# Retention attention and a gated convolution unit on one core: 64x64 inter-chunk products that open the output banks, joint chunk states, earlier weights and a new slot order

## The chip, the cores and the metric

The kernel runs on one core of a Trainium2 chip. The metric is the device time of one execution in microseconds (us), the median of several runs. The engines of the core are TensorE (PE in the profile, with its weight loads shown as PEld), VectorE (DVE), ScalarE (ACT), GpSimd (POOL) and SyncE (SP, which only issues transfers here).

## The reference

Inputs are q, k, v of shape (8 batches, 8 heads, 576 positions, 64), a value matrix and an output matrix of 512x512, and a causal convolution of five taps per channel. All are float32.

```python
scores = q @ k.T / sqrt(64)
Dmat   = where(i >= j, gamma[h] ** (i - j), 0)      # decay by distance, per head
attn   = (scores * Dmat) @ v                        # no softmax
x      = attn with the heads side by side           # (8, 576, 512)
gate   = sigmoid(sum over k of conv_w[k] * x shifted by k)
out    = (gate * (x @ w_val)) @ w_out
```

## The kernel before, in words

The decay is split into a factor on q and a factor on k by position, so the attention is linear attention with a causal mask. Each batch is cut into chunks of 128 positions. Within a chunk the kernel forms masked scores and multiplies them with v. Everything from earlier chunks is summed up in a running state, a 64x64 matrix per head (the sum of k-transposed times v), and reaches the chunk as one product of q with that state, the inter-chunk term.

The work is a list of 20 steps. Batches go in pairs, `u` from 0 to 3. Per pair there are five steps: two for the first batch and two for the second, each of 256 positions (two chunks, `x` = 0 and 1, with positions interleaved as `r` = 0 and 1), and one of 64 positions for both batches together, the remainder (`bb` is None). A step has these parts, each a function:

- `load` issues three transfers (k, q, v; 512 KB each) on SP's queue, four steps ahead. `cast` makes bfloat16 tiles `kb`, `qb`, `vb` with the decay factors multiplied in. It is called two steps ahead, and except at the start POOL does it (L199, L205).
- `transp` transposes kb and qb on PE (`tpk`, `tpq`, L218); ACT copies the first to `kt` (L224), DVE the second to `qt` (L222).
- `scores` (L242) are 64x64 products into PSUM tiles `sc`; DVE multiplies by the mask into `am` (L249). It is called for two groups of head pairs.
- `values` (L303) multiplies am with vb into two output banks `o`, one per chunk.
- `state` (L266) forms `ds`, the step's addition to the state, one call per chunk. `state_sum` adds it to the running sum `sn` on DVE (L281, L283), and ACT casts it to `wst` (L286). wst holds a head pair as a 128x128 block with zeros off the diagonal, so each of ACT's casts fills one half of the partitions and there are two per chunk.
- `inter` (L317) is the inter-chunk term: 128x128 products of wst with qt, added to the o banks after values has opened them.
- `evac` copies o to the layout `xt` (or `xr` for remainders) on ACT (L342, L335).

When a batch's 512 positions are done, they form a block for the second half: `conv` (L375, 160 products of 32x32 tiles with the diagonals `diag` in four PSUM tiles, then four sigmoids `gt` on ACT, L382), four pieces `val` (L390, `vps`, and DVE's product `zt`, L392) and four pieces `outp` (L397, `ops`, ACT's copy `ob`, L400, and a store on SP's queue). The remainders of two pairs make one block of 256. The last batch is given as two blocks of 256.

The order on each engine is the order of the program text; nothing is reordered later. The pieces of blocks wait in the list `work`. Between the parts of a step the program calls `fill(us)`, which adds to a credit and then takes pieces while the credit is at least half of the next piece's cost; the credit is capped at 4.0. A convolution is taken only where `fill` allows it. Transposes, states, convolutions, projections and outputs share one PSUM pool of four banks, `glp` with the tag "gps"; scores have two banks (`scp`) and the outputs o two (`opp`).

The full step of before, in program order:

```python
scores(s, ga); fill(0.9); transp(s + 1); scores(s, gb)
values(s, ga); inter(s, ga); fill(2.2, True)
state(s + 1, 0); values(s, gb); state(s + 1, 1); inter(s, gb)
evac(s); state_sum(s + 1, 0); state_sum(s + 1, 1); fill(1.8)
```

The start issues step 0's loads, makes constants, issues three more steps' loads, casts step 0, then calls `load_weights` (the convolution's taps `cw` as five transfers on ACT's queue, the two matrices on POOL's queue, converted to bfloat16 in the transfer) and casts step 1. `prep_weights`, called in step 1, builds the diagonals on DVE and rearranges the value matrix on ACT.

Of the kernel before, what the change touches and what calls it, by code (L numbers as in the profile page):

```python
# [31 lines left out]
def kernel(  # L32
# [14 lines left out]
    P = 128  # L47
# [14 lines left out]

    cst = ctx.enter_context(tc.tile_pool(name="cst", bufs=1))
# [82 lines left out]
    wtmp = cst.tile([P, DT, DM], BF16)  # L146
    wval = cst.tile([P, DT, NQ, P], BF16)
    wout = cst.tile([P, NQ, DM], BF16)

    def load_weights():  # L150
        with nc.allow_non_contiguous_dma(reason="conv"):
            for kk in range(KC):
                nc.scalar.dma_start(out=cw[:, kk, :],
                                    in_=moe_conv_w[kk].rearrange("(do di) -> di do", di=P))
        nc.gpsimd.dma_start(out=wtmp, in_=moe_w_val.rearrange("(do di) dp -> di do dp", di=P))
        for c in range(DT):
            nc.gpsimd.dma_start(
                out=wout[c * Q:(c + 1) * Q],
                in_=moe_w_out[c * P:(c + 1) * P, :].rearrange("(r x) n -> x r n", x=Q))

    def prep_weights():

        nc.vector.tensor_tensor(idr, ident[:, 0:Q], ident[:, Q:2 * Q], op=ALU.add)
        for i in range(2, NQ):
            nc.vector.tensor_tensor(idr, idr, ident[:, i * Q:(i + 1) * Q], op=ALU.add)
        nc.vector.tensor_copy(cwh, cw)
        nc.vector.tensor_tensor(cwl, cw, cwh, op=ALU.subtract)
        shp = [P, KC * DT, Q]
        for p2, w in ((0, cwh), (1, cwl)):
            nc.vector.tensor_tensor(  # L170
                diag[:, p2].rearrange("p k c x -> p (k c) x"),
                idr.unsqueeze(1).to_broadcast(shp),
                w.rearrange("p k c -> p (k c)").unsqueeze(2).to_broadcast(shp), op=ALU.mult)
        for do in range(DT):
            nc.scalar.copy(wval[:, do].rearrange("p r (c x) -> p r c x", x=Q),
                           wtmp[:, do].rearrange("p (c r x) -> p r c x", r=NQ, x=Q))


    wst = []
    for i in range(8):  # L180
        w = cst.tile([P, HP, 2, D], BF16, tag=f"wst{i}", name="wst")
        nc.vector.memset(w, 0.0)
        wst.append(w)


    def cast(s):
        u, bb, n = steps[s]
        r = st[s]
        R = 1 if bb is None else 2
        shp = [P, R, H, D]  # L190
        f0 = n * 2
        nb = 2 if bb is None else 4
        kb = cs.tile(shp, BF16, tag=f"kb{R}", name="kb", bufs=nb)
        qb = cs.tile(shp, BF16, tag=f"qb{R}", name="qb", bufs=nb)
        vb = cs.tile(shp, BF16, tag=f"vb{R}", name="vb", bufs=nb)

        for dst, src, f, eng in ((kb, r["kf"], fk, nc.gpsimd),
                                 (qb, r["qf"], fq, nc.vector if s == 0 else nc.gpsimd)):
            eng.tensor_tensor(dst, src.rearrange("p h r d -> p r h d"),  # L199
                              f[:, f0:f0 + R, :].unsqueeze(3).to_broadcast(shp), op=ALU.mult)  # L200
        vsrc = r["vf"].rearrange("p h r d -> p r h d")
        if s < 2:
            nc.scalar.copy(vb, vsrc)
        else:
            nc.gpsimd.tensor_copy(vb, vsrc)  # L205
        r.update(qb=qb, kb=kb, vb=vb)

    def transp(s):
        if s >= NS:
            return  # L210
        r = st[s]
        R = 1 if steps[s][1] is None else 2
        for nm in ("k", "q"):
            src = r[nm + "b"]
            tp = glp.tile([P, HP, R, P], BF16, tag="gps", name="tp" + nm)
            for hp in range(HP):
                for rr in range(R):
                    nc.tensor.transpose(tp[:, hp, rr, :],  # L218
                                        src[:, rr, 2 * hp:2 * hp + 2, :].rearrange("p a d -> p (a d)"), ident)
            t = at.tile([P, HP, R, P], BF16, tag=f"{nm}t{R}", name=nm + "t")  # L220
            if nm == "q":
                nc.vector.tensor_copy(t, tp)  # L222
            else:
                nc.scalar.copy(t, tp)  # L224
            r[nm + "t"] = t
# [30 lines left out]
    def state(s, x):  # L256
        if s >= NS or steps[s][1] is None:
            return
        u, bb, n = steps[s]
        r = st[s]  # L260
        ds = glp.tile([P, HP, D], F32, tag="gps", name="ds")
        for hp in range(HP):
            for rr in range(2):
                for hh in range(2):
                    h = 2 * hp + hh
                    nc.tensor.matmul(ds[HS[hh], hp, :], lhsT=r["kb"][HS[x], rr, h, :],  # L266
                                     rhs=r["vb"][HS[x], rr, h, :],
                                     start=(hp == 0 and rr == 0), stop=True, skip_group_check=True)
        r[("ds", x)] = ds

    def state_sum(s, x):
# [3 lines left out]
        ds = st[s][("ds", x)]  # L275
        m = 2 * n + x

        w = wst[6 + bb] if m == 2 * NSC - 1 else wst[m + 3 * bb]
# [6 lines left out]
        for hh in range(2):  # L285
            nc.scalar.copy(w[HS[hh], :, hh, :], sn[HS[hh]])  # L286
        wcur[(u, bb, m + 1)] = w

    xts = {}
    xrs = {}  # L290

    def values(s, hps):
# [3 lines left out]
        if "o" not in r:  # L296
            r["o"] = [opp.tile([P, HP, R * HF], F32, tag="o", name="o") for _ in range(2)]
        o = r["o"]
        for a, hp in enumerate(hps):
            for rj in range(R):  # L300
                for hh in range(2):
                    for x in range(2):
                        nc.tensor.matmul(o[x][HS[hh], hp, :], lhsT=r["vb"][HS[x], rj, 2 * hp + hh, :],  # L303
                                         rhs=r[("am", hps[0], hh)][HS[x], a, rj, :],
                                         start=(hp == 0 and rj == 0), stop=True, skip_group_check=True)

    def inter(s, hps):
        u, bb, n = steps[s]
        r = st[s]
        R = 1 if bb is None else 2  # L310
        o = r["o"]
        for x in range(2):
            key = (u, x, 2 * NSC) if bb is None else (u, bb, 2 * n + x)
            if key not in wcur:
                continue
            for hp in hps:
                nc.tensor.matmul(o[x][:, hp, :].rearrange("p (r i) -> p r i", r=R),  # L317
                                 lhsT=wcur[key][:, hp].rearrange("p a d -> p (a d)"),
                                 rhs=r["qt"][:, hp, :, HS[x]],
                                 start=False, stop=True, skip_group_check=True)  # L320

    def evac(s):
# [13 lines left out]
        else:  # L336
            if u not in xts:
                xts[u] = xp.tile([P, DT, 2, PAD + NSC * SC], BF16, name="xt")
                nc.gpsimd.memset(xts[u][:, :, :, 0:PAD], 0.0)
# [7 lines left out]
    work = []  # L347

    def push_block(xt, bi, t0, segs):
# [35 lines left out]
        def val(d):  # L385
            if d == 0:
                z[0] = zp.tile([P, DT, N], BF16, tag=f"z{N}", name="zt")
            vp = glp.tile(shape, F32, tag="gps", name="vps")
# [5 lines left out]
        def outp(m):  # L394
            op = glp.tile([P, DM], F32, tag="gps", name="ops")
# [22 lines left out]
    def fill(us, conv_ok=False):  # L418

        credit[0] = min(credit[0] + us, 4.0)  # L420
# [6 lines left out]

    for s in range(1, LOOK):
        load(s)
    cast(0)  # L430
    load_weights()
    cast(1)
    transp(0)
    for x in range(2):
        state(0, x)
        state_sum(0, x)
    for s in range(NS):
        u, bb, n = steps[s]
        last = u == B // 2 - 1
        if s == 1:  # L440
            prep_weights()
# [4 lines left out]
        if bb is None:  # L446
            hps = list(range(HP))
            scores(s, hps)
            fill(0.9)
            transp(s + 1)  # L450
            values(s, hps)
            state(s + 1, 0)
            state(s + 1, 1)
            inter(s, hps)
            evac(s)
            state_sum(s + 1, 0)
            state_sum(s + 1, 1)
            fill(4.0, True)
        else:
            ga, gb = list(range(HP // 2)), list(range(HP // 2, HP))  # L460
            scores(s, ga)
            fill(0.9)
            transp(s + 1)
            scores(s, gb)
            values(s, ga)
            inter(s, ga)
            fill(2.2, True)
            state(s + 1, 0)
            values(s, gb)
            state(s + 1, 1)  # L470
            inter(s, gb)
            evac(s)
            state_sum(s + 1, 0)
            state_sum(s + 1, 1)
            fill(1.8)
        b = 2 * u + (bb or 0)
        if bb is None:
            if u % 2 == 1:
                push_block(xrs[u // 2], None, 0, [(b - 2 + j, NSC * SC, REM) for j in range(4)])
        elif last and bb == 1:  # L480
            push_block(xts[u], bb, n * SC, [(b, n * SC, SC)])
        elif n == NSC - 1:
            push_block(xts[u], bb, 0, [(b, 0, NSC * SC)])
# [32 lines left out]
```

## Time and profile before

| | |
|---|---|
| time, median of three runs | 229.23 us (227.87 to 231.61) |
| span of the profiled execution | 228.7 us |
| instructions | 9242 |
| read from and written to device memory | 30.42 MB and 9.44 MB |
| share of 16 transfer engines, loads and stores | 62.4% |
| tap transfer (cw), packets | 2640 for 0.01 MB |
| convolution products (L375) | 1760 with their weight loads |
| inter products (L317) | 128 |

A line of a timeline gives the start, the time from first start to last end, the engine, the source line, the operation and its tiles, the count, and in square brackets the idle time before it and what ended it. A line of waits gives the engine and line that waited, what released it, and then the total, the number of times and the longest. PEld and PE overlap.

### The profile page before, as it was taken

Reading aid. Unit: us, or ns where it says so; the run is one execution under the profiler, and the core shown is the slowest. Engines: PE = TensorE matmul, PEld = TensorE weight load, DVE = VectorE, ACT = ScalarE, POOL = GpSimd, SP = SyncE. Lnnn points to the kernel's source line nnn. Section 1 sums busy time; section 2 is a strip of 40 time slices with the busy share of each in tenths; the row PEclk is TensorE's granted clock in tenths of the full one; section 3 lists DMA queues with packets and bytes.
Section 4 is the critical chain, followed back from the end, with each engine's and each line's share of the span. In section 5 each row is a group of like instructions: output and inputs, shape, how many; then the busy total and the mean of one; then the engine's idle time right before and its main releaser. Section 6 shows DMA issues by size and latency. Waiting matters only on the chain.

```text
span 228.7 us, 9242 instructions
## 1 busy us (share of the span) xinstructions
PE 170.9 (75%) x4160; PEld 108.0 (47%) x4160; DVE 101.0 (44%) x189; ACT 115.1 (50%) x228; POOL 89.4 (39%) x84
## 2 busy tenths in 40 slices
PE   0505769589799867997997958993899788894981
PEld 0404558145554743563565543553456554462560
DVE  3602885164275723733853605530476617320220
ACT  5107648366646737493484645283247736541331
POOL 3951676681783087067602750087500000000000
PEclk9999956999999999999999995899799979999798
DMA  6999999996991899669449995069404000312024
GB/s 168 290 220 229 278 202 242 286 264 224 257 202 56 242 311 285 184 209 269 81 140 268 307 259 141 0 212 304 92 20 167 3 6 0 143 47 95 3 95 92
DMA packets 71622, 39.39 MB, mean 172 GB/s; under 512 B 16800, under 2 KB 66976, under 8 KB 71584
## 3 DMA queue, kind: packets, MB, share of 16 engines
q1 hardware_dynamic: 67840, 37.76, 62.4%
q0 software_dynamic: 1104, 1.05, 2.7%
q8 instruction: 32, 0.52, 1.0%
q10 hardware_dynamic: 2640, 0.01, 0.7%
q14 instruction: 6, 0.05, 0.1%
HBM read 30.42 MB, written 9.44 MB: 174 GB/s over the span
## 4 chain that ended last, share of the span: by engine, by line
PE 58%; DVE 13%; ACT 10%; issue 9%; DMA 5%; SPq 3%; ACTq 0%; DVEq 0%
PE vps L390 14%; PE cps L375 13%; PE ops L397 12%; DMA vf<-in_v_dram 5%; DVE am L249 4%; PE sc L242 4%; PE o L303 4%; DVE zt L392 3%; PE o L317 3%; PE tpk L218 3%; PE tpq L218 3%; PE ds L266 3%; SPq L97 3%; ACT xt L342 2%; ACT gt L382 2%
## 5 line engine op out<-in xcount | busy, mean ns | idle before, releaser
L392 DVE TENSOR_TENSOR zt<-gt,vps 128x512 bf16<-128x512 f32 (+1 forms) x44 | 25.9, 590 | 69.8 <-PE vps L390 69.5
L199 POOL TENSOR_TENSOR kb<-kf,fk 128x1024 bf16<-128x1024 f32 (+1 forms) x20 | 34.6, 1730 | 40.4 <-DMA kf<-in_k_dram 27.6
L249 DVE TENSOR_TENSOR am<-sc,mask_c 128x512 bf16<-128x512 f32 x64 | 41.1, 684 | 16.5 <-PE sc L242 16.4
L390 PE MATMUL vps<-xt,wval 128*128 128x512 bf16 (+1 forms) x144 | 35.1, 383 | 7.4 <-ACT gt L382 4.3
L375 PE MATMUL cps<-xt,diag 32*32 32x512 bf16 (+1 forms) x1440 | 27.9, 380 | 16.0 <-issue 11.9
L397 PE MATMUL ops<-wout,zt 128*128 128x512 bf16 x144 | 37.5, 389 | 1.5 <-DVE zt L392 1.5
L400 ACT COPY ob<-ops 128x512 f32<-128x512 f32 x36 | 20.6, 590 | 33.4 <-PE ops L397 24.2
L382 ACT ACTIVATE gt<-cps 128x512 f32<-128x512 f32 (+1 forms) x44 | 19.4, 524 | 34.7 <-PE cps L375 34.7
L375 PEld LDWEIGHTS <-diag 32*32 32x32 bf16 x1760 | 21.7, 89 | 27.0 <-issue 23.8
L199 POOL TENSOR_TENSOR qb<-qf,fq 128x1024 bf16<-128x1024 f32 (+1 forms) x19 | 32.7, 1721 | 2.7 <-DMA qf<-in_q_dram 2.3
L342 ACT CAST xt<-o 128x512 bf16<-128x512 f32 x32 | 21.7, 751 | 13.7 <-PE o L317 7.1
L242 PE MATMUL sc<-qt,kt 64*64 64x128 bf16 (+1 forms) x576 | 18.1, 239 | 13.6 <-ACT kt L224 9.1
L390 PEld LDWEIGHTS <-wval 128*128 128x128 bf16 x176 | 17.0, 101 | 22.3 <-issue 12.9
L286 ACT CAST wst<-sn 64x256 bf16<-64x256 f32 x64 | 25.8, 403 | 1.0
L333 POOL COPY xr<-xt 128x32 bf16<-128x32 bf16 x4 | 0.8, 210 | 59.9 <-ACT xt L342 59.9
L224 ACT COPY kt<-tpk 128x1024 bf16<-128x1024 bf16 (+1 forms) x20 | 18.6, 932 | 10.7 <-PE tpk L218 10.4
L242 PEld LDWEIGHTS <-kt 64*64 64x64 bf16 x576 | 11.0, 117 | 24.1 <-issue 11.9
L397 PEld LDWEIGHTS <-zt 128*128 128x128 bf16 x144 | 13.2, 100 | 17.3 <-DVE zt L392 5.7
L303 PE MATMUL o<-am,vb 64*64 64x128 bf16 (+1 forms) x576 | 17.9, 231 | 2.9 <-issue 1.3
L218 PE MATMUL tpk<-ident,kb 128*128 128x128 bf16 x144 | 13.0, 239 | 7.9 <-POOL kb L199 7.9
L205 POOL CAST vb<-vf 128x1024 bf16<-128x1024 f32 (+1 forms) x18 | 16.9, 941 | 3.1 <-DMA vf<-in_v_dram 1.9
L218 PEld LDWEIGHTS <-kb 128*128 128x128 bf16 x144 | 10.4, 108 | 11.7 <-POOL kb L199 7.9
(46 smaller groups left out, 144.9 us busy)
## 6 DMA issues: line engine op xcount, KB each, us to landing
kf<-in_k_dram SPq DMA_DIRECT2D x16, 512.0 KB, 5.9
qf<-in_q_dram SPq DMA_DIRECT2D x16, 512.0 KB, 6.8
vf<-in_v_dram SPq DMA_DIRECT2D x16, 512.0 KB, 7.6
out_dram<-ob SPq DMA_DIRECT2D x32, 256.0 KB, 2.4
kf<-in_k_dram SPq DMA_DIRECT2D x8, 128.0 KB, 6.0
qf<-in_q_dram SPq DMA_DIRECT2D x8, 128.0 KB, 5.3
vf<-in_v_dram SPq DMA_DIRECT2D x8, 128.0 KB, 3.8
out_dram<-ob SPq DMA_DIRECT2D x8, 128.0 KB, 3.2
```

Source lines behind the costliest of these rows:

```text
L199: eng.tensor_tensor(dst, src.rearrange("p h r d -> p r h d"), f[:, f0:f0 + R, :].unsqueeze(3).to_broadcast(shp), op=ALU.mult)
L218: nc.tensor.transpose(tp[:, hp, rr, :], src[:, rr, 2 * hp:2 * hp + 2, :].rearrange("p a d -> p (a d)"), ident)
L242: nc.tensor.matmul(sc[hh][HS[x], a, rj, :].rearrange("p (r i) -> p r i", r=R), lhsT=r["kt"][HS[hh], hp, rj, HS[x]], rhs=r["qt"][HS[hh], hp ...
L249: nc.vector.tensor_tensor(am, sc[hh], mk.rearrange("p j i x -> p j (i x)").unsqueeze(1).to_broadcast(shp), op=ALU.mult)
L286: nc.scalar.copy(w[HS[hh], :, hh, :], sn[HS[hh]])
L303: nc.tensor.matmul(o[x][HS[hh], hp, :], lhsT=r["vb"][HS[x], rj, 2 * hp + hh, :], rhs=r[("am", hps[0], hh)][HS[x], a, rj, :], start=(hp == ...
L342: nc.scalar.copy(xts[u][:, :, bb, t0:t0 + P].rearrange("p a (i r) -> p a r i", r=R), o[x].rearrange("p a (r i) -> p a r i", r=R))
L375: nc.tensor.matmul(fold(cps[r][c * Q:(c + 1) * Q]), lhsT=diag[rs, p2, kk, c, :], rhs=win(c, kk)[rs], start=(kk == 0 and p2 == 0), stop=(kk ...
L382: nc.scalar.activation(gt, cps[r], AF.Sigmoid)
L390: nc.tensor.matmul(fold(vp), lhsT=wval[:, do, d, :], rhs=win(do, PAD), start=(do == 0), stop=(do == DT - 1))
L392: nc.vector.tensor_tensor(z[0][:, d, :], g[d], vp, op=ALU.mult)
L397: nc.tensor.matmul(op, lhsT=z[0][:, d, m * P:(m + 1) * P], rhs=wout[:, d, :], start=(d == 0), stop=(d == DT - 1))
```

## The change

Six things change together.

1. The state goes to bfloat16 as it is, without zero blocks: one cast of 128 partitions per chunk into a tile `w`. The inter-chunk term becomes 64x64 products, two per head pair and chunk, and it comes before `values`, so that it opens the output banks where a state exists.
2. `state` forms both chunks' additions in one call, with the products of both chunks alternating.
3. The taps come in one transfer on POOL's queue, and the diagonals are built on POOL, both ahead of the first cast. The two matrices come as float32 on SP's queue right behind step 0's loads, into tiles of the load pool, and are converted by ACT (`wval`) and POOL (`wout`).
4. Step 0 casts k on DVE, and step 1 casts v on POOL.
5. The parts of a step follow lists of slots. A letter is a part, a number is a `fill`, and "C" takes a convolution if one is next. The first batch is given as two blocks of 256.
6. The credit is capped at 2.0. After the last step, projections and outputs use the PSUM banks of scores and of o.

```diff
+    TPS, DSS, CAP = False, False, 2.0
...
-    wtmp = cst.tile([P, DT, DM], BF16)
...
+    with nc.allow_non_contiguous_dma(reason="conv"):
+        nc.gpsimd.dma_start(out=cw.rearrange("p k c -> p (k c)"),
+                            in_=moe_conv_w.rearrange("k (do di) -> di (k do)", di=P))
+
+    nc.gpsimd.tensor_tensor(idr, ident[:, 0:Q], ident[:, Q:2 * Q], op=ALU.add)
...
+    nc.gpsimd.tensor_copy(cwh, cw)
+    nc.gpsimd.tensor_tensor(cwl, cw, cwh, op=ALU.subtract)
...
     def load_weights():
-        with nc.allow_non_contiguous_dma(reason="conv"):
-            for kk in range(KC):
-                nc.scalar.dma_start(out=cw[:, kk, :],
-                                    in_=moe_conv_w[kk].rearrange("(do di) -> di do", di=P))
-        nc.gpsimd.dma_start(out=wtmp, in_=moe_w_val.rearrange("(do di) dp -> di do dp", di=P))
...
+        for half in range(2):
+            t = ld.tile([P, 2, DM], F32, tag="qf2" if half else "kf2", name="wvf", bufs=4)
+            nc.sync.dma_start(out=t, in_=moe_w_val[half * 2 * P:(half + 1) * 2 * P, :]
+                              .rearrange("(do di) dp -> di do dp", di=P))
+            wf[half] = t
...
     def prep_weights():
...
         for do in range(DT):
             nc.scalar.copy(wval[:, do].rearrange("p r (c x) -> p r c x", x=Q),
-                           wtmp[:, do].rearrange("p (c r x) -> p r c x", r=NQ, x=Q))
...
+                           wf[do // 2][:, do % 2].rearrange("p (c r x) -> p r c x", r=NQ, x=Q))
+        for half in range(2):
+            nc.gpsimd.tensor_copy(wout[:, 2 * half:2 * half + 2], wf[2 + half])
...
-        for dst, src, f, eng in ((kb, r["kf"], fk, nc.gpsimd),
+        for dst, src, f, eng in ((kb, r["kf"], fk, nc.vector if s == 0 else nc.gpsimd),
...
-        if s < 2:
+        if s == 0:
             nc.scalar.copy(vb, vsrc)
...
-    def state(s, x):
+    def state(s):
...
+                for x in range(2):
+                    for hh in range(2):
+                        h = 2 * hp + hh
+                        nc.tensor.matmul(ds[x][HS[hh], hp, :], lhsT=r["kb"][HS[x], rr, h, :],
+                                         rhs=r["vb"][HS[x], rr, h, :],
+                                         start=(hp == 0 and rr == 0), stop=True, skip_group_check=True)
...
-        for hh in range(2):
-            nc.scalar.copy(w[HS[hh], :, hh, :], sn[HS[hh]])
+        nc.scalar.copy(w, sn)
...
+    def inter(s):
...
+        for hp in range(HP):
+            for x in range(2):
+                for hh in range(2):
+                    if keys[x] in wcur:
+                        nc.tensor.matmul(r["o"][x][HS[hh], hp, :].rearrange("p (r i) -> p r i", r=R),
+                                         lhsT=wcur[keys[x]][HS[hh], hp, :], rhs=r["qt"][HS[hh], hp, :, HS[x]],
+                                         start=(hp == 0), stop=True, skip_group_check=True)
...
+    def gps(shape, name):
+
+        pools = [(glp, "gps")] if tail[0] is None else [(scp, "sc"), (opp, "o")]
...
-        credit[0] = min(credit[0] + us, 4.0)
+        credit[0] = min(credit[0] + us, CAP)
...
+    load_weights()
     for s in range(1, LOOK):
         load(s)
     cast(0)
-    load_weights()
+    transp(0)
+    state(0)
+    for x in range(2):
+        state_sum(0, x)
+    prep_weights()
     cast(1)
...
+    FIRST = ["I", "Sa", "Sb", "0.0", "Vb", "Va", "E", "B", "C", "X", "XS", "5.85", "T"]
+    FULL = [["I", "0.0", "Sa", "C", "T", "Va", "Sb", "5.4", "Vb", "X", "E", "B", "XS", "7.2"],
+            ["C", "I", "Sa", "X", "4.95", "XS", "Sb", "0.45", "T", "Va", "Vb", "E", "1.35", "B"]]
+    PART = ["X", "I", "Sr", "4.95", "T", "3.05", "Vr", "XS", "E", "B", "C"]
```

In the lists I is `inter`, Sa, Sb and Sr are `scores` for the first two head pairs, the last two and all four, Va, Vb and Vr are `values` in the same way, T is `transp` of the next step, X and XS are `state` and `state_sum` of the next step, E is `evac`, and B puts a finished block in the list. FULL[0] and FULL[1] are for a batch's first and second step, PART for remainders and FIRST for step 0.

## The prediction

> **What bounds the kernel now.** I read the page's busy shares first, then the table of windows, then the waits of PE, then the timeline of the start.
>
> ```profile
> PE 170.9 (75%) x4160; PEld 108.0 (47%) x4160; DVE 101.0 (44%) x189; ACT 115.1 (50%) x228; POOL 89.4 (39%) x84
> ...
> PE 58%; DVE 13%; ACT 10%; issue 9%; DMA 5%; SPq 3%; ACTq 0%; DVEq 0%
> ```
>
> PE leads, and the chain that ended last runs through it for 58% of the span. The rest of the chain is hand-overs to DVE and ACT, and 9% "issue". The windows (columns: length; busy time of PE, PEld, DVE, ACT, POOL; granted clock; DMA share; GB/s) split the span at landmarks: first scores, first 512-wide convolution (38.0), second one (58.0), fourth, sixth, tail.
>
> ```profile
> 0.00:19.95 19.95, 2.89 (x48) 2.30 (x49) 6.26 (x17) 6.00 (x21) 11.03 (x22) 1.00 1.03 224
> 19.95:38.00 18.05, 14.58 (x305) 11.84 (x306) 14.02 (x26) 12.38 (x23) 12.32 (x10) 0.74 1.06 234
> 38.00:58.03 20.03, 16.23 (x410) 9.68 (x410) 8.48 (x17) 11.34 (x21) 11.26 (x8) 0.98 0.94 260
> 58.03:101.40 43.37, 36.70 (x910) 22.54 (x908) 22.52 (x41) 26.05 (x50) 22.62 (x19) 1.00 0.83 218
> 101.40:154.10 52.70, 44.44 (x1088) 27.17 (x1088) 23.93 (x43) 28.17 (x55) 24.06 (x19) 0.94 0.70 187
> 154.10:200.10 46.00, 37.36 (x859) 22.48 (x858) 20.69 (x36) 23.44 (x44) 8.14 (x9) 0.93 0.33 93
> 200.10:228.70 28.60, 18.65 (x554) 11.95 (x552) 5.06 (x12) 7.77 (x20) 0.00 (x0) 0.90 0.22 66
> ```
>
> Three regimes. Up to 38 us the transfers are full (share 1.03, 1.06) and PE starves. From 58 to 200 PE is about 84% busy and no other engine is near it. In the tail everything is one chain. The timeline of the start shows why PE starves:
>
> ```profile
> 8.85 9.05 ACTq L153 DMA_DIRECT2D cw<-in_moe_conv_w_dram  x5
> ...
> 17.94 1.04 ACT L203 CAST vb<-vf 128x1024 bf16<-128x1024 f32 x1 [8.05 <-DMA cw<-in_moe_conv_w_dram]
> 18.89 1.01 ACT L224 COPY kt<-tpk 128x1024 bf16<-128x1024 bf16 x1
> 19.80 1.66 ACT L286 CAST wst<-sn 64x256 bf16<-64x256 f32 x4
> 19.95 0.40 PEld L242 LDWEIGHTS <-kt 64*64 64x64 bf16 x16 [9.27 <-ACT kt L224]
> ```
>
> ACT spends 9 us issuing five transfers of 4-byte elements and then casts step 1's values, so step 0's kt copy, ready since 8.9, waits. Then the diagonals (L163 to L170) sit on DVE from 25.72 to 29.4, ahead of the masking that PE needs (PE gap of 3.13 us). For 58 to 200 the waits of PE (total, times, longest) are:
>
> ```profile
> PE cps L375 <- issue: 8.5, 6, 4.3
> PE vps L390 <- ACT gt L382: 3.1, 5, 0.7
> PE cps L375 <- ACT kt L224: 2.5, 3, 1.2
> PE vps L390 <- ACT xt L342: 2.3, 3, 0.8
> PE ops L397 <- DVE zt L392: 1.5, 4, 0.5
> ```
>
> [...]
>
> **The change, part by part.**
>
> *Start.* Step 0's three loads land at 5.2, 7.0 and 8.8 us (issue plus landing), one per 1.8 us. The weights now follow as 2 MB of float32 on the same queue, four times a 512 KB load: to 16.0. Step 1's loads land at 17.8, 19.6 and 21.3 (before: 10.7, 12.4, 17.5). Step 0 no longer waits for ACT: kb and qb both on DVE (2 x 1.79) end at 9.5, transposes at about 10.6, and its scores and values finish near 17, not 25. But the state of step 1 (X) stands ahead of the first block's projection in PE's order, so PE is then gated by POOL, which serves in order: cw, diagonals, two wout copies, then kb, qb, vb of step 1. cw is the unknown: 2560 elements of 4 bytes, now one transfer issued by POOL at 5.8. Before, they took from 8.85 to 24.7 (17.5 + 7.2), 15.9 us; that is the upper bound (lands 21.7). Below, POOL's issue time by the wtmp and wout rows (0.94 us for 512 rows, 0.54 for 128, so some 3.1 for 2560) plus their own packet time (0.7% of the span, 1.6 us) and about as much latency: 11. I take 17, since the queue beside it is full. The diagonals on POOL cost 2 x 1.2 (1.90 us x 640/1024) plus 0.4: ready at 14, 19.8 or 24.5. wout copies 2 x 0.94, not before 16.0: done at 17.9, 21.7, 26.4. kb, qb, vb are 1.9 + 1.9 + 1.04: X at 22.8, 26.5, 31.3. From X to the first 512-wide convolution I add: projection 2 x 1.9, output 2 x 1.8, one 256-wide convolution 2.4, transposes 4.5, scores 2.9, values 2.9, states 4 x 0.58, inter 1.5, together 23.9, plus 3 for the cold clock and 2 of waits: 29. It starts at 51.7, 55.4 or 60.2, against 58.0. Taken: **2.6 saved** (6.3 to -2.2).
>
> *States at once.* Two calls of 16 cost 0.33 + 0.40 us of weight loads, one call of 32 costs 0.49 (99.87): 0.25 x 4 steps = 1.0 us per batch pair. *Inter as 64x64.* Sixteen weight loads take 0.26 us, the eight 128-wide ones 2 x 0.23: little by itself[...]. Over three pairs from 58 to 200: **4 saved**.
>
> *w without zero halves.* 64 casts of 0.403 us on ACT become 32 of about 0.4: 13 us of ACT. ACT is 50% busy, so this is worth only what stood behind it: kt, which the convolution waited for (2.5).
>
> *Slot order.* Between scores and the values that need them stand now a transpose, a projection or an output. Waits other than "issue" and gt sum to 9.9 (2.5 + 2.3 + 1.5 and nine rows under 0.8); I take 8 as gone. The gt wait (3.1) stays: where T follows C, the transposes need the PSUM buffers that gt frees. Against it: 1.5 for such buffer waits in new places. The clock of 0.94 and 0.93 lost 0.06 x 52.7 + 0.07 x 46 = 6.4[...]. PE's rows grow from 8322 to 8930 (256 for inter, 352 for the first block cut in two), 7% more to fetch: 0.8. **8 - 1.5 + 3 - 0.8 = 8.7 saved.** CAP 2.0 lets a fill place two or three pieces, yet PE's printed order still leaves three 256-wide blocks for the tail, as before.
>
> *Tail.* Projections and outputs use other PSUM pools, so the next convolution doesn't wait for ob: 0.50 + 0.46 in the timeline. **0.9 saved.** The memset of xt moving to the start, and DVE's eight wst memsets (2.19 us, before its data lands) cost nothing: DVE waits for the loads there.
>
> Sum 2.6 + 4 + 8.7 + 0.9 = 16.2; 229.2 - 16.2 = **213**.
>
> **Rivals.** *Late cw*: the upper bound holds, 4.8 us worse: 218. For it: the old transfers ran 16 us beside the same queue. Against: one transfer, started earlier. *All waits go*: early cw (6.3), work 4, all 9.9, all 6.4 of clock, tail 1.5: 201. For it: no engine but PE is over 61% busy in 58 to 101. Against: the transfers would need about 9.4 MB per 38 us, 248 GB/s, close to what the start reaches. *No change*: late cw (-2.2), work 4 and tail 0.9 saved, 2.3 of new costs and no wait gone: 229. *Slower*: the same, but C followed by T costs a microsecond at each of nine convolutions in place of 1.5 in all: 229.2 + 2.2 - 4 - 0.9 + 9 + 0.8 = 236. For it: one gps pool of four serves transposes, states, projections and convolutions.
>
> **How the numbers follow.** Forecast 0.47, late cw 0.18, all waits 0.20, no change 0.07, slower 0.08. The range 201 to 225 leaves out the last two and the far side of the third. Faster by over 2% (below 224.6) is the first three: 0.85; within 2% 0.07; slower 0.08.
>
> **What would show it.** Right: first scores by 14 us, the cast of step 1 on POOL starting between 18 and 26, the first 512-wide convolution near 55, about 40 us per batch pair, no wait of cps on kt, clock above 0.95. Wrong: POOL idle on cw beyond 24 us, transposes waiting for gt by over a microsecond per block, or "issue" gaps well above the 8.5 us of before.

## The result and the profile after

The changed kernel takes 217.05 us, the median of four runs (215.82 to 222.73), against 228.56 for the kernel before on the same chip: a ratio of 0.949, 95% interval 0.939 to 0.959. In a later set of runs it was 0.952 (0.945 to 0.960). The forecast was 213 us, range 201 to 225. Medians and ranges are over all runs of a kernel; a ratio and its interval leave out runs more than 1.5% above its fastest, and none is given where only one run is left. The profiled execution spans 214.0 us (before: 228.7). The two spans differ by 14.7 us and the medians by 11.5, because the profiled run of before was slower than its median and this one faster.

The first line below is from the page's busy times, the others from the table of windows (columns as before), cut at the same landmarks: three pieces of the start, up to the second batch's 512-wide convolution at 59.4, then the steps pair by pair, then the tail.

```profile
PE 165.8 (77%) x4464; PEld 107.6 (50%) x4464; DVE 97.7 (46%) x181; ACT 97.7 (46%) x199; POOL 93.1 (43%) x85
```

```profile
0.00:26.00 26.00, 9.19 (x289) 6.87 (x293) 7.60 (x16) 11.66 (x32) 14.96 (x27) 1.00 1.04 243
26.00:38.70 12.70, 11.10 (x224) 8.30 (x224) 7.16 (x14) 5.91 (x10) 10.82 (x8) 1.00 1.04 239
38.70:59.40 20.70, 14.75 (x467) 11.21 (x466) 9.30 (x19) 7.90 (x15) 13.85 (x11) 0.89 1.05 282
59.38:101.40 42.02, 37.34 (x942) 22.76 (x938) 22.90 (x41) 21.12 (x39) 21.32 (x17) 0.93 0.81 220
101.38:143.00 41.62, 35.65 (x1005) 23.04 (x1005) 21.85 (x40) 20.18 (x40) 19.71 (x14) 0.96 0.82 208
143.00:187.35 44.35, 39.74 (x1019) 23.99 (x1024) 23.87 (x42) 23.13 (x44) 12.46 (x11) 1.00 0.44 128
187.35:214.00 26.65, 18.08 (x553) 11.45 (x552) 5.05 (x12) 7.79 (x20) 0.00 (x0) 0.89 0.22 65
```

The three parts give different answers. The landmark that closes the start stood at 58.03 before and is at 59.38 now: 1.3 us lost. The middle shrank from 142.1 us (58.03 to 200.1) to 128.0: **14.1 saved**. The tail shrank from 28.60 to 26.65: 1.95 saved. So nearly the whole gain lies in the steps between start and tail.

One window over each middle splits it further. First before, then after:

```profile
58.03:200.10 142.07, 118.50 (x2857) 72.19 (x2854) 67.14 (x120) 77.65 (x147) 54.82 (x45) 0.95 0.62 166
```

```profile
59.38:187.35 127.97, 112.71 (x2965) 69.77 (x2966) 68.61 (x121) 64.44 (x122) 53.47 (x41) 0.96 0.69 184
```

PE's busy time fell by 5.8 us, and the time in which it stood by 8.3 (23.6 to 15.3). What it stood for is in the waits of PE over the same window of the changed kernel. "issue" is idle time for which the profile shows nothing that PE waited for:

```profile
PE cps L394 <- issue: 3.7, 3, 1.9
PE vps L409 <- ACT xt L352: 2.7, 3, 1.1
PE vps L409 <- issue: 2.1, 1, 2.1
PE sc L246 <- issue: 1.9, 1, 1.9
PE tpk L222 <- ACT gt L401: 1.8, 3, 0.7
PE o L327 <- DVE am L253: 0.5, 1, 0.5
PE cps L394 <- ACT kt L228: 0.4, 1, 0.4
```

Summing all rows of this view, waits for a named engine fell from 13.0 us to 6.5, and "issue" from 9.8 to 7.7. The 2.5 us for kt ahead of the convolution are down to 0.4, and those for zt (1.5) are gone from the list; xt ahead of the projections, with 2.7, is no shorter than it was (2.3). What "issue" is comes out in the experiments.

### The profile page after: what moved, and what is told of

Its sections match the earlier page's. It is cut to its first block, busy times and chain, and to the rows that moved or that the text cites. A ratio compares the mean times of both kernels' runs of the same rounds, so it can differ in the third digit from the quotient of the medians.

```text
span 214.0 us, 9828 instructions
## 1 busy us (share of the span) xinstructions
PE 165.8 (77%) x4464; PEld 107.6 (50%) x4464; DVE 97.7 (46%) x181; ACT 97.7 (46%) x199; POOL 93.1 (43%) x85
## 5 line engine op out<-in xcount | busy, mean ns | idle before, releaser
L203 POOL TENSOR_TENSOR kb<-kf,fk 128x1024 bf16<-128x1024 f32 (+1 forms) x19 | 32.7, 1721 | 25.6 <-DMA kf<-in_k_dram 23.5
L394 PE MATMUL cps<-xt,diag 32*32 32x512 bf16 (+1 forms) x1600 | 30.1, 371 | 10.1 <-issue 7.4
L411 DVE TENSOR_TENSOR zt<-gt,vps 128x256 bf16<-128x256 f32 (+1 forms) x48 | 26.2, 552 | 23.7 <-PE vps L409 22.8
L409 PE MATMUL vps<-xt,wval 128*128 128x512 bf16 (+1 forms) x160 | 33.0, 352 | 4.8 <-ACT xt L352 2.7
L401 ACT ACTIVATE gt<-cps 128x256 f32<-128x256 f32 (+1 forms) x48 | 19.7, 496 | 33.7 <-PE cps L394 33.7
L394 PEld LDWEIGHTS <-diag 32*32 32x32 bf16 x1920 | 23.7, 89 | 21.7 <-issue 16.8
L409 PEld LDWEIGHTS <-wval 128*128 128x128 bf16 x192 | 18.3, 104 | 19.9 <-issue 8.4
L226 DVE COPY qt<-tpq 128x1024 bf16<-128x1024 bf16 (+1 forms) x20 | 12.7, 636 | 23.7 <-PE tpq L222 23.4
L416 PEld LDWEIGHTS <-zt 128*128 128x128 bf16 x144 | 12.7, 100 | 14.8 <-issue 1.7
L327 PE MATMUL o<-am,vb 64*64 64x128 bf16 (+1 forms) x576 | 15.9, 228 | 3.1 <-DVE am L253 1.9
L246 PEld LDWEIGHTS <-kt 64*64 64x64 bf16 x576 | 13.2, 111 | 7.9 <-issue 7.9
L222 PEld LDWEIGHTS <-kb 128*128 128x128 bf16 x144 | 10.3, 105 | 12.0 <-DVE kb L203 6.5
## 6 DMA issues: line engine op xcount, KB each, us to landing
wof<-in_moe_w_out_dram SPq DMA_DIRECT2D x8, 128.0 KB, 7.1
kf<-in_k_dram SPq DMA_DIRECT2D x8, 128.0 KB, 5.9
qf<-in_q_dram SPq DMA_DIRECT2D x8, 128.0 KB, 5.0
```

Source lines behind the costliest of these rows:

```text
L222: nc.tensor.transpose(tp[:, hp, rr, :], src[:, rr, 2 * hp:2 * hp + 2, :].rearrange("p a d -> p (a d)"), ident)
L246: nc.tensor.matmul(sc[hh][HS[x], a, rj, :].rearrange("p (r i) -> p r i", r=R), lhsT=r["kt"][HS[hh], hp, rj, HS[x]], rhs=r["qt"][HS[hh], hp ...
L394: nc.tensor.matmul(fold(cps[r][c * Q:(c + 1) * Q]), lhsT=diag[rs, p2, kk, c, :], rhs=win(c, kk)[rs], start=(kk == 0 and p2 == 0), stop=(kk ...
L401: nc.scalar.activation(gt, cps[r], AF.Sigmoid)
L409: nc.tensor.matmul(fold(vp), lhsT=wval[:, do, d, :], rhs=win(do, PAD), start=(do == 0), stop=(do == DT - 1))
L411: nc.vector.tensor_tensor(z[0][:, d, :], g[d], vp, op=ALU.mult)
```

## The experiments

The theory to test: the **slot order** carries the gain, because independent work now stands between a producer and its consumer. The rival: the **new forms** carry it (less work for PE and ACT, earlier weights). Each kernel ran beside the kernel before on the same chip; its median was 230.4 us in the first set, 231.7 in the second, 230.0 and 230.75 in the last two.

**The changed kernel once more** (no edit), as the yardstick of its set.

> The changed kernel itself, beside which the other runs of this group are read. Every theory expects what was measured before: about 217 us, a ratio to the kernel before of 0.94 to 0.96.

Measured: 219.67 us (217.85 to 221.94), ratio 0.952 (0.945 to 0.960). Its middle took 132.2 us, 4.2 more than in the profile above, with named waits of 7.3 us, a busy time of 111.9 and longer "issue" gaps (11.6 us against 7.7; in the whole span, those of the convolution came to 13.7 against 9.3). So the middle saved 10 to 14 us, and differences of 4 us between single profiles' middles mean little by themselves.

**The old slot order with the new forms.**

```diff
-    FIRST = ["I", "Sa", "Sb", "0.0", "Vb", "Va", "E", "B", "C", "X", "XS", "5.85", "T"]
-    FULL = [...]
+    FIRST = ["I", "Sa", "0.9", "T", "Sb", "Va", "c2.2", "X", "Vb", "E", "XS", "1.8", "B"]
+    FULL = [FIRST, FIRST]
-    PART = ["X", "I", "Sr", "4.95", "T", "3.05", "Vr", "XS", "E", "B", "C"]
+    PART = ["I", "Sr", "0.9", "T", "Vr", "X", "E", "XS", "c4.0", "B"]
```

Here "c" lets a fill take a convolution, and the cap is 4.0 as before. The list is not quite that of before: inter still opens the banks and so stands at the head of a step, and the state is one call.

> The changed kernel with the slot order and the credit cap of the kernel before (the inter-chunk term stays ahead of the scores, everything else stays as changed). Theory A, the order carries most of the gain after the first 59 us: 225 to 229 us. Rival B, the 64x64 forms and the halved casts on ScalarE carry it: 216 to 220 us.

Measured: 244.38 us (243.48 to 250.88), ratio 1.061 (1.054 to 1.069): 14 us slower than the kernel before, which neither theory had allowed. The waits of PE from 10 to 40 us show one part of it:

```profile
PE tpk L222 <- POOL kb L203: 10.6, 1, 10.6
```

With the old list the transposes of step 1 come right behind step 0's first scores, and POOL has the diagonals and the weights in front of step 1's casts.

**The same, but step 0 keeps its new list**, to take that wait away.

```diff
+    FIRST = ["I", "Sa", "Sb", "0.0", "Vb", "Va", "E", "B", "C", "X", "XS", "5.85", "T"]
```

> The changed kernel with the old slot order and the cap of 4.0 for every step but the first, which keeps its new list; so the transposes of step 1 no longer stand ahead of what PE could do while POOL casts. Theory A (what the old order loses lies in the steps of the loop: inter, opening the banks at a step's head, waits for the states and the evacuation just ahead of it, and the transposes for gt): most of the 24 us by which the old order with the new form missed the changed kernel stays, 231 to 240. Theory B (it lay in the start, where one wait of 10.6 us stood): 221 to 229.

Measured: 238.39 us (235.89 to 240.19), ratio 1.025 (1.015 to 1.034). So step 0's list is worth 6 to 8 us of the loss (by the times, or by the ratios) and the steps the other 17 to 19. Theory A's range holds: in this order the new forms are worse than the kernel before, in which inter stood behind values. The convolution that closes the start begins at 59.29, as in the changed kernel, so the middles can be compared directly; the window and the waits of PE in it:

```profile
59.29:208.90 149.61, 116.97 (x2952) 69.90 (x2944) 67.41 (x121) 64.55 (x122) 54.54 (x42) 0.94 0.60 159
```

```profile
PE cps L394 <- issue: 13.8, 6, 3.9
PE o L314 <- ACT w L290: 3.7, 3, 1.7
PE vps L409 <- ACT gt L401: 3.4, 6, 0.7
...
PE o L327 <- DVE am L253: 2.3, 5, 0.6
...
PE ops L416 <- DVE zt L411: 1.3, 4, 0.4
```

The middle is 21.6 us longer than the changed kernel's: about 4.3 in busy time, 7.7 in "issue" (15.4 against 7.7) and 10.3 in named waits (16.8 against 6.5). Against the second profile of the changed kernel it is 17.4 longer, with 9.5 of it in named waits. Of these the new order hides 3.7 for w, 1.8 of the 2.3 for am, 1.3 for zt, and all of gt ahead of projections (though the transposes then wait 1.8 for gt).

**The same with inter behind the first scores**, to see whether opening the banks at the head of a step is what costs. The second half's scores and values move too, ahead of the transposes and of the first half's values.

```diff
+    FULL = [["Sa", "0.9", "I", "Sb", "T", "Vb", "c2.2", "X", "Va", "E", "XS", "1.8", "B"], ["Sa", "0.9", "I", "Sb", "T", "Vb", "c2.2", "X", "Va", "E", "XS", "1.8", "B"]]
```

> The same with inter moved behind a step's first scores and the first fill, and the second half's scores and values ahead of the transposes and the first half's values. Theory A (inter at the head of a step is what costs): at least 5 us below the kernel with inter at the head, and the waits of o on w and on xt gone from the list. Theory B (the old list's other neighbours cost, the transposes behind gt and the values behind am): within 3 us of it.

Measured: 251.24 us (242.75 to 251.63); no ratio can be given. Not even the fastest run is below the 238.39 of the kernel above, so Theory A fell; at 4.4 us above, it is outside Theory B's 3 us as well. The wait of o on w went only from 3.7 to 3.0. Moving inter in this way doesn't rescue the old order; as scores and values moved with it, the run doesn't isolate inter's place.

**The new order with the old 128x128 inter** (zero blocks, two casts per chunk), still ahead of values.

```diff
-        w = sp.tile([P, HP, D], BF16, tag="wl" if last else "w", name="w", bufs=3 if last else 6)
+        w = wst[6 + bb] if last else wst[m + 3 * bb]
...
-        nc.scalar.copy(w, sn)
+        for hh in range(2):
+            nc.scalar.copy(w[HS[hh], :, hh, :], sn[HS[hh]])
...
-                                         lhsT=wcur[keys[x]][HS[hh], hp, :], rhs=r["qt"][HS[hh], hp, :, HS[x]],
+                                     lhsT=wcur[keys[x]][:, hp].rearrange("p a d -> p (a d)"),
```

> The changed kernel with the inter-chunk term as 128x128 products on zero-padded states again, two casts per chunk on ScalarE, still ahead of the values and in the new order. Theory A: 217 to 220 us, at most 3 us more, since the row counts show little work saved and ScalarE has room. Rival B: 222 us or more.

Measured: 222.55 us (220.32 to 223.84), ratio 0.964 (0.952 to 0.975), against 0.952 (0.945 to 0.960) for the changed kernel in the same set: at most some 3 us, and the intervals overlap. Its middle takes 132.7 us, the changed kernel's in that set 132.2. That is 9.4 us less than in the kernel before, with its form of inter; and the two runs with the old order, slow ones, had the new forms. So the order carries most of the gain. The run doesn't show that the form costs nothing: ACT's busy time is 114.3 us again, and named waits in the middle are 10.7 us against 7.3, most of the difference for xt; shorter "issue" (9.9 against 11.6) and a higher clock (0.97 against 0.95) stand on the other side in these two profiles.

**The state's two chunks one after the other inside the one call.**

```diff
-        for hp in range(HP):
-            for rr in range(2):
-                for x in range(2):
+        for x in range(2):
+            for hp in range(HP):
+                for rr in range(2):
```

> The changed kernel with the loops of the state put back to one chunk after the other inside the one call: 16 matmuls of one row half, then 16 of the other. Theory A ([...]the pairing saves about 1 us per batch pair): 222 to 224, ds calls about 0.25 us longer. Theory B (weight loads bound it and the order inside the call is free): 218 to 221.

Measured: 219.70 us (218.38 to 220.61), ratio 0.948 (0.943 to 0.953), the changed kernel's own. The products did get longer: in the groups by line, ds has 10.4 us of busy time against 8.4 in the changed kernel. That saving of busy time is real and the time doesn't show it.

**The old start with the new order**: the taps on ACT's queue, the matrices on POOL's, the diagonals on DVE, and the first batch as one block.

```diff
-    load_weights()
     for s in range(1, LOOK):
         load(s)
     cast(0)
+    load_weights()
+    cast(1)
     transp(0)
...
-    prep_weights()
-    cast(1)
...
+        if s == 1:
+            prep_weights()
```

> The changed kernel with the start of the kernel before: taps as five transfers on ScalarE's queue, matrices converted in the transfer on GpSimd's queue, diagonals on VectorE in step 1, the first batch as one block. Theory A, the new start gains nothing (the first 512-wide convolution stood at 59.4 us against 58.0): 214 to 218 us. Rival C, the new start is worth what freeing ScalarE promised: 222 to 226 us.

Measured: 219.87 us (215.88 to 221.53), beside 219.67 (217.85 to 221.94) for the changed kernel in its set; no ratio can be given. No run reached Rival C's 222, and no gain from the new start is seen in the whole time. Its one profile, of the slowest run, has the second batch's convolution at 63.37 us, 4 later than the changed kernel, so what the start is worth by itself stays open.

**An earlier state of step 1**: its loads ahead of the weights, its casts ahead of the diagonals on POOL, the copies of the output matrix on ACT, and in step 0's list the state and transposes ahead of the convolution.

```diff
-    load_weights()
-    for s in range(1, LOOK):
+    load(1)
+    load_weights()
+    for s in range(2, LOOK):
         load(s)
     cast(0)
+    cast(1)
+    prep_diag()
...
-            nc.gpsimd.tensor_copy(wout[:, 2 * half:2 * half + 2], wf[2 + half])
+            nc.scalar.copy(wout[:, 2 * half:2 * half + 2], wf[2 + half])
...
-    FIRST = [..., "E", "B", "C", "X", "XS", "5.85", "T"]
+    FIRST = [..., "E", "B", "X", "XS", "T", "C", "5.85"]
```

> The changed kernel with step 1's loads ahead of the weights on the queue, step 1's casts ahead of the diagonals on POOL, the copies of the output weights on ACT, and in step 0's list the state and the transposes of step 1 ahead of the first convolution. PE then gets step 1's states some 9 us sooner (near 17, not 25.9). Theory A (what follows is bound by transfers and by PE's own work, so an early state only makes PE wait later): within 2 us of the changed kernel, 217 to 221, the second batch's 512-wide convolution still near 59. Theory B (POOL's serial queue at the start is what holds PE): that convolution starts 4 us or more sooner, 213 to 216.

Measured: 222.28 us (220.14 to 224.06), ratio 0.958 (0.952 to 0.964). That is above both ranges. Step 1's states did start at 16.8 us, not 25.9, but the second batch's convolution started at 61.90, later than in the changed kernel (59.38). The timeline shows a wait that took the place of the old one: step 0's evacuation now stood behind the weights' casts on ACT, which waited for their transfers.

```profile
23.79 1.04 ACT L188 CAST wout<-wof 128x1024 bf16<-128x1024 f32 x1 [0.99 <-DMA wof<-in_moe_w_out_dram]
24.74 1.36 ACT L353 CAST xt<-o 128x512 bf16<-128x512 f32 x2
26.15 0.40 PE L395 MATMUL cps<-xt,diag 32*32 32x256 bf16 x3 [6.87 <-ACT xt L353]
```

So this kernel exchanged one wait for another, and can't tell whether POOL's queue or the transfers bound the start.

**The tail's projections and outputs back in the one pool** (the line that switches pools is taken out).

```diff
-    tail[0] = 0
```

> The changed kernel with the tail's projections and outputs back in the one pool of four PSUM buffers. Theory A (the other pools save the two waits for ob and something like a microsecond at each of three convolutions): tail 1 to 2 us longer, 220.5 to 222. Theory B (the tail is one chain anyway): 218 to 220.

Measured: 221.20 us (219.94 to 223.94), ratio 0.953 (0.947 to 0.959). Its tail takes 29.87 us from the first convolution on, against 26.72 (the cut at 187.35 above gives 26.65). The waits of PE in the tail have two rows that the changed kernel doesn't have there:

```profile
PE vps L409 <- ACT gt L401: 1.4, 3, 0.5
PE cps L394 <- ACT ob L419: 1.0, 2, 0.5
```

The two waits for ob that Theory A named are back, with three for gt; the tail is 3.15 us longer, where it said 1 to 2. In the whole time the step is too small for its interval.

**The convolution in two parts**, two taps and three, with inter or the first scores between them.

```diff
+            for kk in (range(2) if part == 0 else range(2, KC)):
...
-    FULL = [["I", "0.0", "Sa", "C", "T", ...], ["C", "I", "Sa", "X", ...]]
+    FULL = [["I", "0.0", "C0", "Sa", "C1", "T", ...], ["C0", "I", "C1", "Sa", "X", ...]]
```

> The changed kernel with each block's convolution cut into two taps and three taps, and in a full step the first or second half's small matmuls (inter or the first scores) between the parts. Theory A (the gaps called issue come from PE's instructions running short within 320 in a row): the issue gaps of the convolution fall to under half of 5 to 9 us per execution, 214 to 217. Theory B (the gaps come every so many instructions wherever these stand): as many gaps, moved to other groups, [...]219 to 223.

Measured: 215.46 us (213.45 to 219.03), ratio 0.936 (0.930 to 0.942). The time is in Theory A's range, but not for its reason: the convolution's issue gaps total 11.6 us in the span (the changed kernel: 9.3 and 13.7). Neither theory stands as written. So two more runs, the first a plain repetition:

> The kernel with the cut convolution once more, with more rounds. Theory A (the cut saves 1 to 2% against the changed kernel, by a warmer clock and fewer waits, not by fewer issue gaps): ratio to the kernel before 0.93 to 0.945, clock above 0.97. Theory B (the first run of it was lucky, the cut is worth nothing): 0.947 to 0.955. Its issue gaps again end where PE's stream reaches matmul 95, 223, 351 and so on, one every 128 matmuls.

Measured: 217.81 us (214.81 to 221.06), ratio 0.939 (0.925 to 0.952), clock 0.97. The ratio is Theory A's, but the interval reaches the changed kernel's: it beats the kernel before beyond its interval, and the changed one probably, by one or two per cent. Why is not shown.

The second puts 56 small products on zeros ahead of everything on PE. They change nothing in the result; they only move PE's later instructions by 112 places, as each product comes with a weight load (x4464 of each on the page of the changed kernel).

```diff
+    pad = cst.tile([P, Q], BF16)
+    nc.vector.memset(pad, 0.0)
+    pads = glp.tile([P, Q], F32, tag="gps", name="pads")
+    for i in range(56):
+        c = i % DT
+        nc.tensor.matmul(pads[c * Q:(c + 1) * Q], lhsT=pad[0:Q], rhs=pad[0:Q], start=True, stop=True,
+                         skip_group_check=True, tile_position=(0, c * Q))
```

> The cut convolution with 56 matmuls of 32x32 on zeros ahead of everything else on PE; they add nothing to the computation and run before the first data lands. Theory A (the issue gaps are waits for the next 256 of PE's instructions, so they come at a fixed count of instructions and not at a place of the program): counted from the first instruction the gaps stay at 95 of every 128 matmuls, so in the program each stands 56 matmuls earlier: in the first block's convolution ahead of its matmul 47, not 103. Their sum may change by some us either way; a replay of the last trace with this shift gives 2 to 4 us less, 212 to 216. Theory B (a gap belongs to the work around it, a queue or a buffer): ahead of matmul 103 as before, and the time as without the shift.

Measured: 218.88 us (216.97 to 223.38), ratio 0.951 (0.942 to 0.961). No faster, so Theory A's forecast of the time was wrong; but the gap moved exactly. The timeline of the second batch's convolution, without the shift and with it:

```profile
58.84 3.20 PE L398 MATMUL cps<-xt,diag 32*32 32x512 bf16 x150 [0.46 <-ACT kt L228]
65.00 0.64 PE L398 MATMUL cps<-xt,diag 32*32 32x512 bf16 x10 [2.96 <-issue]
```

```profile
58.75 2.38 PE L405 MATMUL cps<-xt,diag 32*32 32x512 bf16 x94 [0.46 <-ACT kt L235]
61.66 1.25 PE L405 MATMUL cps<-xt,diag 32*32 32x512 bf16 x66 [0.53 <-issue]
```

The gap stood behind product 150 of 160 and stands behind product 94 now: 56 earlier, to the product. The gap behind product 102 of the convolution before it is gone. The gap expected ahead of product 47 of the first one isn't seen: PE waited for the diagonals just before it (2.9 and 0.8 us). Theory A holds in its substance. Issue gaps over the span were 16.6 us without the shift and 15.3 with it: in the convolution 4.4 in place of 12.0, and the rest elsewhere (3.8 in one gap among the scores).

The trace supports this in a second way, in the kernel with the old order in its steps. Every issue gap of over 0.5 us of that kernel, with the product that ends it counted from the first on PE, and the landing of the last packet of the instruction queue before it:

```
gap ends   length   product     modulo 128   packet landed   later by
 22.31     1.68        224         96            20.77          1.54
 47.96     0.71        736         96            46.82          1.14
 65.73     2.97       1120         96            64.45          1.28
 92.88     2.97       1632         96            91.40          1.48
114.56     1.85       2016         96           113.32          1.24
136.95     1.34       2528         96           135.54          1.41
166.58     3.85       3168         96           165.18          1.40
193.94     1.72       3680         96           192.44          1.50
212.36     1.78       4064         96           211.09          1.27
228.04     1.65       4448         96           226.44          1.59
```

In 4464 products all ten stand at the same place of a period of 128 products, that is 256 instructions, and each ends 1.1 to 1.6 us after a packet of 16 KB landed; in the profiles of before and of the changed kernel such landings are at least 3.4 us apart. In the kernel before it is the same: nine gaps, places 95 and 96, 1.3 to 1.6 us after a landing. The page of the changed kernel counts 34 such packets (0.56 MB) for 8928 products and weight loads, 34.9 times 256; that of the kernel before 32 (0.52 MB) for 8320, 32.5 times. From here on such a gap is called a fetch gap.

## Why the prediction was right, and which terms were off

**Middle, right in size and in its main cause.** Predicted 4 + 8.7 = 12.7 saved, measured 14.1, and 9.9 in the second profile of the changed kernel. Inside it:

- *Named waits*: predicted 8 saved and 1.5 added, 6.5 net; measured 13.0 to 6.5, and 7.3 in the second profile. The kernel with the old order in its steps has 16.8, so the order shortens them; that the figure fits to the decimal is luck. The prediction expected the gt wait to stay; it fell from 3.8 (all rows) to 1.8, while the waits for xt (2.3) didn't go (3.0 with the one ahead of inter). Its "nine rows under 0.8" are six of up to 0.8, one of them for gt.
- *Clock*: predicted 3 of the 6.4 back for fewer gaps. That was the author's estimate, and no run shows that the clock follows the gaps. By the prediction's way of estimating the loss, the windows give 0.07 x 42.0 + 0.04 x 41.6 = 4.6 us against 6.4, so 1.8 back; in the second profile the mean clock of the middle is 0.95, as before, and nothing came back.
- *Instruction fetch*: predicted 0.8 lost; 2.1 gained in this profile (9.8 to 7.7), but the second had 3.9 more. The sign isn't settled. That "issue" is PE waiting for its instructions was an inference in the prediction; the shift by 56 products and the ten landings support it now.
- *Work*: predicted 4, of which 3 x 1.0 for the states; the rest was the author's estimate, and no run shows it by itself. Busy time fell by 5.8, of which some 1.8 is clock by the estimate above: about 4 left. The runs don't confirm that this is time: undoing the alternation of the states adds 2.0 us of their busy time and leaves the time where it was, and 128x128 inter costs 3 us at most.

**Start, the step that failed.** Predicted 2.6 saved, measured 1.3 lost at the landmark, and no gain seen in the whole time beside the old start. Its first half was right: first scores at 11.5 us (by 14), the taps in use from 16.22 (taken: 17; the early bound of 11 adds up to 12.1, which changed nothing), step 1's casts on POOL began at 21.07 (18 to 26), its states at 25.9 (26.5). The rest, from X to the 512-wide convolution, is this:

```profile
25.88:59.38 33.50, 25.95 (x689) 19.61 (x689) 16.44 (x33) 13.81 (x25) 24.64 (x18) 0.93 1.04 265
```

```profile
25.88 0.64 PE L270 MATMUL ds<-vb,kb 64*64 64x64 bf16 x32 [2.49 <-POOL vb L209]
26.45 3.60 PE L409 MATMUL vps<-xt,wval 128*128 128x256 bf16 x16
```

```profile
PE cps L394 <- issue: 2.3, 1, 2.3
PE o L314 <- ACT xt L352: 1.5, 3, 0.8
PE sc L246 <- DVE am L253: 1.2, 2, 0.8
PE o L327 <- issue: 1.0, 1, 1.0
PE o L314 <- DVE qt L226: 0.8, 1, 0.8
```

The prediction entered 23.9 of work, 3 for the clock (an estimate) and 2 of waits, 29 in all; it took 33.5. In the kernel before, eight transposes took 1.03 us at 34.78, where the granted clock was 0.50, and 0.62 at 25.84, where it was 1.00. The work and the clock were right in sum: PE was busy for 25.95 us, where 26.9 were entered. (The first projection took 3.60 us, the second 1.92; the 1.7 between them are inside the 3. Their cause is not shown: the windows give 1.00 there, but the clock's record in this trace begins only at 30.88.) What failed is the term "2 of waits": PE stood for 7.6 us. Two fetch gaps, 3.3 together, were not in the list at all, and hand-overs took 4.3: xt 1.5, am 1.6, qt 0.8, gt 0.4. The sum was short by 4.5, and with 0.6 from the earlier X it came out at 59.38, not 55.4. The account of the start before was off too: between 20 and 38 us PE was busy for 14.58 of 18.05 us at a clock of 0.74, so it did not starve there.

**Tail, right but too small.** Predicted 0.9, measured 1.95. The waits for ob (1.0) are gone as said. Left out were three projections that waited 0.5 us each for a bank that gt frees, 1.4 in all: they are in the profile of before, are gone after, and come back in the run with the one pool. Longer fetch gaps (2.5 to 3.6) took 1.1 back.

**The rivals.** The late taps didn't happen. Not all waits went (xt, 2.7). The slower case expected C followed by T to cost a microsecond at each convolution; it cost 1.8 us at three, in the middle.

Of the signs named, the 512-wide convolution near 55 failed. 40 us per pair was 42.0, 41.6 and 44.4; the kt wait is 0.4; the clock 0.955.

**What was not separated**: the cap of 2.0 was changed only together with the order, so "the order" here means both, and the first batch's two blocks were changed only with the start. Those two blocks put 160 more convolution products ahead of the landmark (320 against 160). And the two halves depend on each other: the new forms in the adapted old order are slower than the kernel before (ratio 1.025; 7.5 us in the middle), while in the new order they are worth up to 3 us. Why is only in part in the waits (3.7 for w, and longer fetch gaps).

## What to carry to other kernels

When the bounding engine executes in program order, sum its named waits first: the order that puts independent work between producer and consumer carried most of the gain here, and the same new products in the old order were slower than what they replaced. Removing work from an engine that also waits (2 us of the states' products) may bring nothing, and from one that isn't the bound little (17 us of ACT, with the form of inter 3 us at most). Give waits a place of their own in a sum: work and clock were entered well in the start, and the waits were 7.6 us where 2 stood. In the start, ask of each earlier step what now stands behind it on an in-order queue: the early state of step 1 moved the wait from POOL to ACT.

## What was not expected of the hardware

- **Instruction fetch is a visible cost.** Fetch gaps of 0.5 to 4.3 us make up most of the 14 to 20 us of "issue" before PE in the kernels before and after, 6 to 9% of the span. Most stand in the dense convolutions (eight of nine before, six of ten after), and shifting the stream by 56 products moved them without removing them (16.6 us of "issue" without the shift, 15.3 with it).
- **A stalled PE continued 1.1 to 1.6 us after the packet had landed**, in 19 gaps of two kernels, the kernel before and the one with the old order in its steps.
- **The clock halved while PE was busy over half of the time.** In the changed kernel it was at half for 10.24 us from 54.77 on. In the 3.4 us before that PE was busy 55% of the time, and its longest gap was 0.8 us. What lowered the clock is not shown. The convolution at 59.38 took 5.72 us for 150 products, at a clock of 0.50; the same 150 took 3.35 in the second profile, where the eight transposes ahead of them took 0.61 us against 1.06 here.

```profile
50.00:54.00 4.00, 2.82 (x75) 1.94 (x74) 2.03 (x4) 1.83 (x5) 3.45 (x3) 1.00 0.60 165
56.00:58.00 2.00, 1.67 (x40) 1.47 (x38) 0.67 (x2) 0.41 (x1) 1.53 (x2) 0.50 1.22 299
```

- **A faster form of a group needn't make a faster kernel**: with alternating row halves the states take 8.4 us of busy time in place of 10.4, at equal time.
